# Four input loads moved earlier on the SyncE queue of a convolution and maxout kernel

## The chip, the core and the metric

The kernel runs on one core of a Trainium2 chip. The metric is the device time of one execution in microseconds. The kernel before took 485.3 us, the median of 11 runs that lay between 483.31 and 487.07.

The core has five engines that matter here: TensorE (PE in the profile, with its weight loads as PEld), VectorE (DVE), ScalarE (ACT), GpSimd (POOL) and SyncE (SP), which only issues transfers. Each takes its instructions in the order in which the program wrote them. An instruction that waits holds up all that stands behind it on the same engine.

## The reference

The input x has 8 batches of 4160 rows of 192 values. Each of 8 heads (24 columns) is filtered along the rows by 7 weights, which are the softmax of that head's row of `weight`. The result goes through a maxout layer with 768 hidden units and an output matrix:

```
w = softmax(weight)                        # 8 heads x 7 taps
y[b, s, h, :] = sum_k w[h, k] * xpad[b, s + k, h, :]      # 6 zero rows ahead of each batch
h = max(max(y @ w1, y @ w2), y @ w3)       # 33280 x 768
out = h @ w_out                            # 33280 x 192, float32
```

## The kernel before

The 33280 rows are cut into 65 blocks of 512. 64 of them lie within one batch; the last is made of the eight remainders of 64 rows. Blocks are numbered t.

The way of one block through the core:

- `load_x(t)` (line 133) brings x to SBUF as float32, in chunks of 112 rows that overlap, so that each holds the rows its filter needs. It is one transfer of 420 KB, or two (168 and 252 KB) where the block begins a batch, as blocks 0 and 8 do. All loads are issued by SyncE. Blocks 0 to 5 have buffers of two small pools of their own; from block 6 on the loads go round the four buffers of `xfp`.
- `cast_x(t)` (line 149) turns it to float16 on GpSimd.
- `conv(t)` (line 295) does the filter as 40 small matmuls with a band matrix, into two PSUM tiles.
- `evac(t, i)` (line 335) copies the two PSUM tiles to SBUF as `ys`, one by ScalarE and one by VectorE.
- `repack(t)` (line 348) puts the heads' columns in order by six SBUF to SBUF transfers, `yd<-ys`, three issued by SyncE and three by GpSimd.
- `double(t)` (line 354) copies the 64 filled partitions to the other 64 by one transfer of 192 KB, `yd<-yd`, issued by SyncE. It must wait until all six pieces have landed.
- `l1(t, j)` (lines 365 to 370), for j from 0 to 5, is the first layer for 128 hidden units: six matmuls, a Relu on ScalarE, a maximum on VectorE. It reads both halves of `yd`.
- `st2(t, u)` (line 409) is the second layer in six parts, and `store` (line 435) writes the result.

Blocks 0 to 2 are treated otherwise: their casts leave gaps for heads so that the convolution gives the right columns at once (`conv_dense`, line 314). Block 2's duplicate is made by two transfers that SyncE issues at lines 482 and 483, once its convolution has been copied out of PSUM.

No scheduler reorders anything: the order of calls in the source is the order on each engine. After a start-up part written out by hand, the loop `for t in range(2, NB)` (line 508) runs iteration t: the first layer of block t mixed with the second layer of block t - 1. On even t it also runs the convolutions of blocks t + 3 and t + 4, and in the first few iterations small tables say which blocks are loaded, cast, convolved, repacked and doubled: iteration 2 convolves blocks 4 and 5, iteration 3 block 6, iteration 4 blocks 7 and 8. From iteration 4 on `load_x(t + 6)` opens each iteration, and must wait for a cast to free its buffer. In iterations 2 and 3 the loads of the table `loads_at` stand behind the repacks:

```
    loads_at = {2: (7,), 3: (8, 9)}
    casts_at = {2: (6,), 3: (7, 8)}
    convs_at = {2: (4, 5), 3: (6,)}
    repacks_at = {2: (4,), 3: (5, 6)}
    doubles_at = {2: (), 3: (4,), 4: (5, 6)}
```

Of the kernel before, what the change touches and what calls it, by code (L numbers as in the profile page):

```python
# [27 lines left out]
def kernel(  # L28
# [84 lines left out]
    def load_x(t, eng=nc.sync):  # L113
        if not 0 <= t < NB:
            return
        chunks = chunks_of[t]
        n = len(chunks)
        pool, tag = (xfp, "xf") if t > 5 else ((xap, "xa") if t in (0, 3, 5) else (xbp, "xb"))
        xf = (pool.tile([P, NQ, D], FP32, tag=tag, name=f"xf_{t}") if n <= NQ else
              const.tile([P, n, D], FP32, name=f"xf_{t}"))  # L120
        parts = []
        i, n = 0, len(chunks)
        row = [c[1] * SEQ + c[2] for c in chunks]
        while i < n:
            k = i
            while (k + 1 < n and chunks[k + 1][3] == chunks[i][3]
                   and row[k + 1] - row[k] == row[i + 1] - row[i]):
                k += 1
            step = row[i + 1] - row[i] if k > i else 0
            rlen = chunks[i][3]  # L130
            src = bass.AP(tensor=x.tensor, offset=row[i] * D,
                          ap=[[D, rlen], [step * D, k - i + 1], [1, D]])
            eng.dma_start(out=xf[0:rlen, i:k + 1, :], in_=src)
            if parts and parts[-1][0] == rlen:
                parts[-1] = (rlen, parts[-1][1], k + 1)
            else:
                parts.append((rlen, i, k + 1))
            i = k + 1
        xin[t] = [xf, None, parts]
# [48 lines left out]
    load_x(1)  # L188
    load_w(2)
    nc.sync.dma_start(out=wos[:], in_=moe_w_out.rearrange("(j p) c -> p j c", p=P))  # L190
    for t in range(2, 6):
        load_x(t)

    ident = const.tile([P, P], FP32)
# [146 lines left out]
    def repack(t):  # L341


        if t >= NB:
            return
        yd = dense[t] = ydp.tile([P, NC, NBLK], FP16, tag="yd", name=f"yd_{t}")
        for n, (half, s0, c, r0, rows) in enumerate(pieces):
            (nc.sync, nc.gpsimd)[n % 2].dma_start(out=yd[r0:r0 + rows, c, :],  # L348
                                                  in_=slots[t][s0:s0 + rows, half, :])

    def double(t):

        if NDENSE <= t < NB:
            nc.sync.dma_start(out=dense[t][HALF:P, :, :], in_=dense[t][0:HALF, :, :])

    def l1(t, j):


        N, y = blkN[t], dense[t]
        ps = [pool.tile([P, NBLK], FP32, tag=tag, name=f"l{tag}_{t}_{j}")  # L360
              for pool, tag in ((psp, "p"), (psq, "q"))]
        for c in range(NC):
            for i in range(2):
                row = slice(HALF * i, HALF * (i + 1))
                nc.tensor.matmul(ps[i][:, 0:N], lhsT=wd[row, c, P * j:P * (j + 1)],  # L365
                                 rhs=y[row, c, 0:N],
                                 start=(c == 0), stop=(c == NC - 1))
        r = rp.tile([P, NBLK], FP16, tag="r", name=f"r_{t}_{j}")
        nc.scalar.activation(out=r[:, 0:N], in_=ps[0][:, 0:N], func=AF.Relu)  # L369
        nc.vector.tensor_max(out=hs[t][:, j, 0:N], in0=r[:, 0:N], in1=ps[1][:, 0:N])  # L370
# [110 lines left out]
    conv_dense(2, (nc.scalar.copy, nc.vector.tensor_copy, nc.scalar.copy), PQ)  # L481
    nc.sync.dma_start(out=dense[2][HALF:P, 0:NC:2, :], in_=dense[2][0:HALF, 0:NC:2, :])
    nc.sync.dma_start(out=dense[2][0:HALF, 1, :], in_=dense[2][HALF:P, 1, :])
    l1(1, 4)
    st2(0, 2, NJ)
    st2(0, 3, NJ)
# [4 lines left out]
    cast_x(4)  # L491
    cast_x(5)
    repack(3)
    load_x(6)
    double(3)
    l1(1, 5)
    st2(0, 4, NJ)
# [2 lines left out]

    loads_at = {2: (7,), 3: (8, 9)}
    casts_at = {2: (6,), 3: (7, 8)}
    convs_at = {2: (4, 5), 3: (6,)}
    repacks_at = {2: (4,), 3: (5, 6)}
# [62 lines left out]
```

The softmax here doesn't subtract the row's maximum and nothing guards it: scores larger than these inputs give would overflow.

## Time and profile before

| what | value |
|---|---|
| median of 11 runs | 485.3 us |
| the profiled execution's own time | 485.75 us |
| its span, first to last instruction | 483.8 us |
| TensorE busy | 468.4 us (97%) |
| VectorE, ScalarE, GpSimd busy | 76%, 67%, 44% |
| mean granted clock of TensorE | 0.992 |
| x loads, 420 KB each: median from issue to landing | 4.8 us |
| `yd<-yd` of 192 KB: median from issue to landing | 3.4 us |

The span is measured in one profiled execution; every time of a row is counted from its start. In a row of the table of groups, the first number after the bar is the time that the group was busy, the second the mean duration in nanoseconds, and after the next bar stands the time that the engine sat idle just before, with what ended it. "PEclk" or the granted clock is the share of TensorE's full clock that it was given. In a row of a timeline stand the start, the duration (of all that was merged in the row), the engine, the line, the operation, the tile written and read, the count, and in brackets the idle time before it. A DMA row on SPq or POOL is the issue of a transfer; it lands later. Matmuls are pipelined, so a busy TensorE is not one at its peak.

### The profile page before, as it was taken

The page shows a single profiled execution, that of the slowest core. Times are in us where ns is not written, and L with a number is a line of the kernel's source. Part 1 is how long each engine was busy: PE and PEld are TensorE (multiplying, and loading weights), DVE is VectorE, ACT ScalarE, POOL GpSimd, SP SyncE. Part 2 cuts the span into 40 slices and gives each one's busy share as a digit, 9 for nine tenths or more (in the row PEclk, how much of TensorE's full clock was granted, in tenths as well). Part 3 has the DMA queues.
Part 4 walks back from the last instruction along what each step waited for, and adds up shares of the span by engine and source line. Part 5 has one row for each costly group of instructions (what it writes and reads, how often), then busy time and mean ns, then how long its engine had stood idle before and what let it go on. Part 6 is the DMA issues. An engine that isn't in the chain of part 4 may idle for free.

```text
span 483.8 us, 21790 instructions
## 1 busy us (share of the span) xinstructions
PE 468.4 (97%) x9008; PEld 392.3 (81%) x9008; DVE 368.8 (76%) x612; ACT 323.8 (67%) x602; POOL 213.4 (44%) x346
## 2 busy tenths in 40 slices
PE   8799799999999999999999999999999999999996
PEld 4377588888888888888888888888888888888995
DVE  7777377778777787778787778777787778787774
ACT  4666376767676767676676766676766676666764
POOL 3644354345345534543554345345525543454200
PEclk9999799999999999999999999999999999999999
DMA  9746866676666667666666676575657766664423
GB/s 193 178 137 164 222 161 173 180 202 164 166 181 184 171 161 201 175 177 173 172 186 170 176 200 168 161 203 155 182 160 182 188 180 181 176 181 115 104 66 99
DMA packets 68576, 81.86 MB, mean 169 GB/s; under 512 B 9422, under 2 KB 57486, under 8 KB 68478
## 3 DMA queue, kind: packets, MB, share of 16 engines
q1 hardware_dynamic: 55310, 49.51, 41.5%
q0 software_dynamic: 13008, 30.88, 20.7%
q8 instruction: 70, 1.15, 1.1%
q14 instruction: 28, 0.23, 0.2%
q10 hardware_dynamic: 160, 0.10, 0.1%
HBM read 30.31 MB, written 25.56 MB: 115 GB/s over the span
## 4 chain that ended last, share of the span: by engine, by line
PE 94%; DVE 2%; ACT 1%; DMA 1%; issue 0%; SPq 0%; POOL 0%; ACTq 0%; POOLq 0%; DVEq 0%
PE lp L365 31%; PE po L409 30%; PE lq L365 25%; PE G L295 7%; DMA xf<-in_x_dram 1%; PE D L314 1%; DVE h L370 1%; ACT r L369 0%; PE idle L211 0%; DVE line L228 0%; ACT L225 0%; DVE wd L250 0%; PE band_cols L232 0%; DVE yd L330 0%; POOL x L149 0%
## 5 line engine op out<-in xcount | busy, mean ns | idle before, releaser
L370 DVE TENSOR_TENSOR h<-r,lq 128x512 f16<-128x512 f16 x390 | 267.1, 685 | 101.3 <-ACT r L369 101.0
L369 ACT ACTIVATE r<-lp 128x512 f16<-128x512 f32 x390 | 232.9, 597 | 141.0 <-PE lp L365 92.8
L365 PE MATMUL lp<-yd,wd 64*128 64x512 f16 x1170 | 316.9, 378 | 2.0 <-DVE wd L250 1.6
L365 PE MATMUL lq<-yd,wd 64*128 64x512 f16 x1170 | 315.8, 376 | 1.7 <-DVE h L370 1.7
L409 PE MATMUL po<-wo,h 64*128 64x192 f16 x3120 | 231.5, 243 | 0.0
L409 PEld LDWEIGHTS <-h 64*128 64x128 f16 x3120 | 186.9, 94 | 26.0 <-issue 0.5
L365 PEld LDWEIGHTS <-wd 64*128 64x128 f16 x2340 | 164.6, 94 | 26.7 <-issue 4.7
L435 POOL DMA_DIRECT2D out_dram<-o x63 | 49.9, 792 | 232.8 <-DVE o L419 221.7
L348 POOL DMA_DIRECT2D yd<-ys x186 | 94.0, 509 | 4.6 <-ACT ys L335 2.1
L409 PE MATMUL po<-m,yd 64*128 64x192 f16 x780 | 87.4, 244 | 0.0
L419 DVE TENSOR_TENSOR o<-a,po 128x384 f32<-128x384 f32 (+1 forms) x132 | 71.4, 542 | 0.6 <-ACT a L418 0.6
L149 POOL CAST x<-xf 112x960 f16<-112x960 f32 x61 | 60.7, 995 | 11.9 <-DMA xf<-in_x_dram 11.9
L418 ACT COPY a<-po 128x384 f32<-128x384 f32 (+1 forms) x132 | 61.6, 468 | 1.4 <-PE po L409 1.4
L409 PEld LDWEIGHTS <-yd 64*128 64x128 f16 x780 | 54.9, 94 | 8.5
L295 PEld LDWEIGHTS <-x 112*32 112x32 f16 x2440 | 29.4, 97 | 18.1 <-issue 13.3
L335 DVE CAST ys<-G 128x512 f16<-128x512 f32 x62 | 39.8, 682 | 5.0 <-PE G L295 5.0
L295 PE MATMUL G<-band,x 112*32 112x103 f16 (+1 forms) x2440 | 34.5, 210 | 4.6 <-POOL x L149 4.6
L335 ACT CAST ys<-G 128x512 f16<-128x512 f32 x62 | 33.6, 588 | 6.8 <-PE G L295 5.5
L166 POOL CAST xz<-xf 112x240 f16<-112x240 f32 (+2 forms) x12 | 3.6, 346 | 7.7 <-DMA xf<-in_x_dram 7.7
L211 PE MATMUL idle<-idle 128*128 128x512 f16 x10 | 4.6, 629 | 1.2 <-DVE idle L206 1.2
L314 PEld LDWEIGHTS <-xz 112*32 112x32 f16 x180 | 3.6, 111 | 1.4 <-DVE w3s L254 0.8
L314 PE MATMUL D<-band,xz 112*32 112x103 f16 (+1 forms) x180 | 4.1, 236 | 0.0
(48 smaller groups left out, 43.1 us busy)
## 6 DMA issues: line engine op xcount, KB each, us to landing
out_dram<-o POOLq DMA_DIRECT2D x63, 384.0 KB, 4.0
xf<-in_x_dram SPq DMA_DIRECT2D x57, 420.0 KB, 4.8
yd<-yd SPq DMA_DIRECT2D x62, 192.0 KB, 3.4
yd<-ys SPq DMA_DIRECT2D x62, 48.0 KB, 3.6
yd<-ys POOLq DMA_DIRECT2D x62, 48.0 KB, 3.6
xf<-in_x_dram SPq DMA_DIRECT2D x8, 252.0 KB, 3.4
yd<-ys SPq DMA_DIRECT2D x62, 32.0 KB, 3.3
yd<-ys POOLq DMA_DIRECT2D x62, 32.0 KB, 3.9
```

Of the source, the lines that this page charges most:

```text
L149: nc.gpsimd.tensor_copy(out=v[0:rl, q0:q1, :], in_=xf[0:rl, q0:q1, :])
L295: nc.tensor.matmul(G[i][32 * g:32 * g + 32, lo:hi], lhsT=x16[0:rlen, cb:cb + 32], rhs=band[0:rlen, h, cc:cc + hi - lo], start=True, stop=T ...
L314: nc.tensor.matmul(ps[32 * g:32 * g + 32, lo:hi], lhsT=xz[t][0:rlen, q, v, 32 * s:32 * s + 32], rhs=band[0:rlen, h, cc:cc + hi - lo], star ...
L335: copy(out=slots[t][:, i, :], in_=convs[t][i][:])
L348: (nc.sync, nc.gpsimd)[n % 2].dma_start(out=yd[r0:r0 + rows, c, :], in_=slots[t][s0:s0 + rows, half, :])
L365: nc.tensor.matmul(ps[i][:, 0:N], lhsT=wd[row, c, P * j:P * (j + 1)], rhs=y[row, c, 0:N], start=(c == 0), stop=(c == NC - 1))
L369: nc.scalar.activation(out=r[:, 0:N], in_=ps[0][:, 0:N], func=AF.Relu)
L370: nc.vector.tensor_max(out=hs[t][:, j, 0:N], in0=r[:, 0:N], in1=ps[1][:, 0:N])
L409: nc.tensor.matmul(ps[b0, i][:, s % 2, :], lhsT=a, rhs=b, start=first, stop=last)
L418: nc.scalar.copy(out=a[:, ss, :], in_=ps[s0, 0][:, ss, :])
L419: nc.vector.tensor_add(out=outs[t][:, s0:s + 1, :], in0=a[:, ss, :], in1=ps[s0, 1][:, ss, :])
L435: qs[i].dma_start(out=bass.AP(tensor=out.tensor, offset=r * D, ap=[[D, n], [step * D, s1 - s0], [1, D]]), in_=ob[p0:p0 + n, s0:s1, :])
```

## The change

Four loads are issued earlier on SyncE. The load of x6 comes directly after x5's. The load of x7 comes after the two transfers of lines 482 and 483, ahead of `repack(3)`. The load of x8 stands where x6's was, between `repack(3)` and `double(3)`. The load of x9 stands where x7's was, behind `repack(4)` in iteration 2. Iteration 3 loads nothing any more. No instruction is added or taken away, and the casts, convolutions and everything on the other engines keep their order.

```diff
-    for t in range(2, 6):
+    for t in range(2, 7):
         load_x(t)
...
     nc.sync.dma_start(out=dense[2][0:HALF, 1, :], in_=dense[2][HALF:P, 1, :])
+    load_x(7)
     l1(1, 4)
...
     repack(3)
-    load_x(6)
+    load_x(8)
     double(3)
...
-    loads_at = {2: (7,), 3: (8, 9)}
+    loads_at = {2: (9,)}
```

## The prediction

> **What bounds the kernel now.** I began with the page's table of groups, and there with the column of idle time. TensorE is busy 97% of the span, and of its matmul groups only the convolution of line 295 sat idle for microseconds; the cast of line 149 ended that idle time.
>
> ```profile
> L295 PE MATMUL G<-band,x 112*32 112x103 f16 (+1 forms) x2440 | 34.5, 210 | 4.6 <-POOL x L149 4.6
> ```
>
> The view of waits from 26 us to the end has that wait of 4.6 us once, and no other matmul row in it. So behind the start-up TensorE never stops except there, and what is won or lost on TensorE comes out at the end one for one. The timeline of TensorE shows the place (start, duration, what, count, idle time before it):
>
> ```profile
> 31.87 1.10 PE L295 MATMUL G<-band,x 112*32 112x103 f16 x80
> ...
> 35.45 0.38 PE L365 MATMUL lp<-yd,wd 64*128 64x512 f16 x1
> ...
> 38.63 0.38 PE L365 MATMUL lp<-yd,wd 64*128 64x512 f16 x1
> ...
> 46.73 0.64 PE L295 MATMUL G<-band,x 112*32 112x103 f16 x40
> 52.01 1.05 PE L295 MATMUL G<-band,x 112*32 112x103 f16 x40 [4.64 <-POOL x L149]
> ...
> 57.04 0.38 PE L365 MATMUL lp<-yd,wd 64*128 64x512 f16 x1
> ```
>
> At 31.87 block iteration 2 runs its two convolutions (blocks 4 and 5) in one piece. At 46.73 iteration 4 runs the same pair for blocks 7 and 8: block 7's forty matmuls end at 46.73 + 0.64 = 47.37, block 8's start at 52.01. The chain of work that ended last, between 46 and 53 us, says why:
>
> ```profile
> 46.90 0.58 SPq L133
> ...
> 47.53 3.29 DMA xf<-in_x_dram
> ...
> 50.96 1.00 POOL x L149
> ```
>
> x8 (in two transfers, being cut at a batch's end) was issued only at 46.90 and 47.53, landed at 50.82, and its cast ended at 51.96. Why so late is read on SyncE's own timeline, which issues in program order:
>
> ```profile
> 14.46 8.84 SPq L133 DMA_DIRECT2D xf<-in_x_dram  x4
> 28.20 0.63 SPq L482 DMA_DIRECT2D yd<-yd  x1
> 28.93 0.56 SPq L483 DMA_DIRECT2D yd<-yd  x1
> 30.29 1.85 SPq L348 DMA_DIRECT2D yd<-ys  x3
> 32.18 0.60 SPq L133 DMA_DIRECT2D xf<-in_x_dram  x1
> 35.67 0.51 SPq L354 DMA_DIRECT2D yd<-yd  x1
> ...
> 41.52 5.33 SPq L348 DMA_DIRECT2D yd<-ys  x6
> 46.90 2.15 SPq L133 DMA_DIRECT2D xf<-in_x_dram  x4
> 49.22 1.23 SPq L354 DMA_DIRECT2D yd<-yd  x2
> ```
>
> x8's load stands behind the six moves of blocks 5 and 6 (41.52 to 46.85), the last of which wait for block 6's evacuation. x6 went at 32.18, x7 at 38.14, so the prefetch is one place too short by iteration 4. The stretches of 4 us show the second cost, in the column after POOL's (granted clock):
>
> ```profile
> 48.00:52.00 4.00, 0.00 (x0) 0.00 (x0) 0.06 (x1) 0.00 (x0) 1.04 (x2) 0.66 0.89 230
> 52.00:56.00 4.00, 4.00 (x68) 2.96 (x70) 1.38 (x3) 1.18 (x2) 2.74 (x5) 0.50 1.05 262
> 56.00:60.00 4.00, 4.00 (x61) 2.95 (x57) 2.77 (x5) 2.16 (x4) 0.38 (x1) 0.99 0.65 188
> ```
>
> TensorE does nothing, its clock falls to half, and stays there until 56.1 after it resumes.
>
> **The change part by part.** It adds no instruction; it moves four loads, five DMA issues, on SyncE. All four buffers of the pool are empty at the start, so none of x6 to x9 waits for a cast; x10 waits for x6's cast as before.
>
> *What is removed.* Take the same stretch in both iterations, from the pair's first matmul to the group l1 3: iteration 2 took 35.45 - 31.87 = 3.58 us, iteration 4 took 57.04 - 46.73 = 10.31. The difference, 6.73 us, is the whole price: 4.64 idle and 2.09 of half clock (conv 8 took 1.05 where iteration 2's second half took 1.10 - 0.64 = 0.46, so 0.59; from the pair's end to l1 3, 57.04 - 53.06 = 3.98 against 35.45 - 32.97 = 2.48, so 1.50). Both iterations step by 1.06 us per group after that, so nothing more is hidden there.
>
> *x8, to the place of x6.* It is issued after repack(3), at 32.18 and about 32.8. x6 took 4.5 us from there, so x8 is in by about 37. What is late next is GpSimd: its queue holds x8's cast behind x7's, which runs 44.26 to 45.25 after the moves of blocks 5 and 6. x8's cast then ends at 46.25; conv 8 can start at 47.37. It is hidden by 1.1 us. x9 takes x7's place at 38.14; its own cast comes in iteration 4 and its convolution in iteration 6, no risk.
>
> *x6, behind x5.* x5's issue ends at 23.30, SyncE then waits until 28.20 for conv 2: x6's issue (about 0.6 us) fits with 4 us to spare. In 27 to 29 us the DMA engines are nearly idle in the windows (16 and 0 GB/s), so x6 is in at 28 to 29.3 (x5, the one just before, took 4.8 us from issue, and x4 to x5 was 1.9 us). Next behind it are the two moves of dense 2, landed at 30.60 and 30.95 for the group at 31.08. Cost 0 to 0.4 us; I take 0, since their packets start near 29.3.
>
> *x7, between the moves of dense 2 and repack(3).* SyncE is free from 29.49 to 30.29, the issue takes 0.6: nothing on SyncE. But its 420 KB now run ahead of repack(3). That repack's last pieces landed at 35.6 and 35.4, and only then could double(3) go, at 35.67. The first group of iteration 3 reads it at 38.63 without waiting. This duplicate has no landing in the trace; others of line 354 took 2.7 us at least, so it was in between 38.37 and 38.63: **at most 0.26 us of cover.** [...] The row: a load such as x6 has 4.5 us from issue to landing, so x7 is in at about 34.0, and the pieces (80 KB, landing at best 2.0 us after issue) follow within half a microsecond, still ahead of 35.6. [...] By the row it is 0 to 0.6. I take 0.3: the rate between 31 and 34 us was 50 to 133 GB/s, where 380 was reached at 35, so there is room for it; the other half of the repack goes by GpSimd's queue.
>
> *Iteration 4's SyncE.* x8 and x9 are gone from it, so x10 goes at 46.90, double(5) at about 47.5, double(6) at about 48.3, when repack(6) has landed (48.2). With the stall gone, iteration 5's first group is at 46.73 + 1.10 + 0.36 + 5.30 = 53.49 (the last two are the gap and the run l1 1 to the next iteration's l1 0 of iteration 2). double(5) lies behind x10 in the queue: x10 in at 51.4 (4.5 us) to 52.7 (5.8, as x9 took among others), then 192 KB at 230 GB/s, 0.8 us: 52.2 to 53.5. Cost 0 to 0.3 us; with it as slow as double(6) was (7.7 us), 1.7. I take 0.1.
>
> *The sum.* 6.73 - 0.3 - 0.1 = 6.3 us. The profiled execution took 485.75 us (span 483.8 and 1.95 around it): 485.75 - 6.3 = 479.4. It lay 0.45 above the median of the runs, so against the median 485.3 - 6.3 = **479.0 us**, 1.3% less.
>
> *The clock.* [...] The rows say 2.09, and that the clock was down by 49.3, 1.9 us after TensorE stopped (0.64 granted between 49 and 50). [...]
>
> **The rivals.**
> *A, the forecast:* the stall goes, new waits sum to under 1 us: 478.5 to 479.6. For it: the one wait of the waits view, and 1.1 us of cover behind it.
> [...]
> *C, no change:* x8's cast is held by something else on GpSimd, and conv 8 waits as long. 485.3. Against it: GpSimd stood idle for 5.71 us ahead of that cast, waiting for the load alone.
> *D, slower:* x7 ahead of repack(3) delays its landing by a whole load, 2.3 us, so double(3) goes at 37.9, and behind x8 it takes 7.7 us as double(6) did: 45.6, 7.0 us after 38.63. That idle time drops the clock too, 2.1: 485.3 - 6.7 + 9.1 = 487.7. It decides from a wait of 4.7 us at iteration 3. Against it: at 36 to 38 us one load, not three, is in the queue.
>
> **How the numbers follow.** A 0.74, B 0.19, C 0.03, D 0.04. Two tenths of a percent (1.0 us) is about what a measurement of this kernel can tell from no change; A and B are faster by more: 0.93. Same 0.03, slower 0.04. The range begins at 485.3 - 6.9 - 0.6 = 477.8 (no new wait, and a median half a microsecond off, as the eleven runs from 483.31 to 487.07 let it be) and ends at 481.6, within B.
>
> **What would show it.** Right: the matmul row of line 295 loses its 4.6 us; the pair of iteration 4 stands as one row of 80, as in iteration 2; the granted clock stays at full from 48 to 56 us; the cast of line 149 no longer waits 5.7 us for its load. [...] Wrong: a wait above 1.9 us before iteration 3's first group with half clock after it, or GpSimd's cast of x8 ending later than 47.4.

## The result and the profile after

The changed kernel took 480.13 us, the median of 12 runs between 478.63 and 482.77. The ratio to the kernel before, run in the same rounds, is 0.9896, with a 95% interval of 0.988 to 0.9911: about 5.0 us, or 1.0%, faster. The forecast was 479.0 us with a range of 477.8 to 481.6.

The profiled execution took 479.65 us, its span is 477.8. In the page's table of groups, the convolution has lost its idle time, and the cast waits for loads 4.2 us in all where it waited 11.9:

```profile
L149 POOL CAST x<-xf 112x960 f16<-112x960 f32 x61 | 60.6, 995 | 4.2 <-DMA xf<-in_x_dram 4.2
...
L295 PE MATMUL G<-band,x 112*32 112x103 f16 (+1 forms) x2440 | 33.9, 209 | 0.0
```

TensorE's timeline, at the places that the prediction named (start, duration, what, count, idle time before it):

```profile
31.58 1.10 PE L295 MATMUL G<-band,x 112*32 112x103 f16 x80
...
39.32 0.64 PE L295 MATMUL G<-band,x 112*32 112x103 f16 x40
...
46.45 1.10 PE L295 MATMUL G<-band,x 112*32 112x103 f16 x80
...
50.03 0.38 PE L365 MATMUL lp<-yd,wd 64*128 64x512 f16 x1
...
54.35 0.39 PE L365 MATMUL lq<-yd,wd 64*128 64x512 f16 x1 [0.77 <-DMA yd<-ys]
```

Blocks 7 and 8 are convolved in one piece of 80. From there to the group l1 3 it takes 50.03 - 46.45 = 3.58 us, the figure of iteration 2 to the hundredth. But the last row is a wait that the kernel before did not have, in iteration 5's first group, which reads block 5's duplicate. The row names a piece of a repack as what ended it; the piece that landed then, issued at 49.82, is of block 7, which this group does not read. I take the wait to be for the duplicate. SyncE's timeline shows that duplicate in its new company:

```profile
41.27 5.79 SPq L348 DMA_DIRECT2D yd<-ys  x6
47.15 0.53 SPq L133 DMA_DIRECT2D xf<-in_x_dram  x1
48.21 1.56 SPq L354 DMA_DIRECT2D yd<-yd  x2
```

The load of x10 is issued at 47.15, the duplicates of blocks 5 and 6 behind it at 48.21 and 48.93. The granted clock (the column after POOL's) stays full:

```profile
48.00:52.00 4.00, 4.00 (x63) 3.04 (x61) 3.23 (x6) 2.44 (x6) 2.71 (x5) 1.00 0.81 244
52.00:56.00 4.00, 3.23 (x49) 2.33 (x46) 2.38 (x5) 2.09 (x4) 0.93 (x2) 1.00 0.83 220
```

In these two profiles the span falls by 6.0 us, in the medians the time falls by about 5.0.

### The profile page after: what moved, and what is told of

Its sections match the earlier page's. It is cut to its first block, busy times and chain, and to the rows that moved or that the text cites. A ratio compares the mean times of both kernels' runs of the same rounds, so it can differ in the third digit from the quotient of the medians.

```text
span 477.8 us, 21790 instructions
## 1 busy us (share of the span) xinstructions
PE 466.6 (98%) x9008; PEld 390.0 (82%) x9008; DVE 367.8 (77%) x612; ACT 323.9 (68%) x602; POOL 213.5 (45%) x346
## 3 DMA queue, kind: packets, MB, share of 16 engines
q8 instruction: 70, 1.15, 1.1%
## 4 chain that ended last, share of the span: by engine, by line
PE 95%; DVE 2%; ACT 1%; DMA 1%; issue 0%; ACTq 0%
PE lp L365 31%; PE po L409 30%; PE lq L365 26%; PE G L295 7%; DMA yd<-ys 1%; PE D L314 1%; DVE h L370 0%; PE idle L211 0%; ACT r L369 0%; DVE wd L250 0%; ACT L225 0%; PE band_cols L232 0%; DVE yd L330 0%; DVE line L228 0%; ACT w3s L254 0%
## 5 line engine op out<-in xcount | busy, mean ns | idle before, releaser
L250 DVE TENSOR_TENSOR wd<-ws,w3s 128x768 f16<-128x768 f32 (+1 forms) x4 | 3.4, 854 | 1.2 <-DMA ws<-in_moe_w_dram 1.1
```

## The experiments

To compare profiles I use one measure, taken from the rows of line 295 in TensorE's timeline: the way from the start of the convolutions of blocks 4 and 5 to that of blocks 9 and 10. It covers iterations 2 to 5, and its parts are A (to block 6's convolution), B (from there to block 7's) and C (from block 7's on). "Loss" is what the whole way took above 28.80 us, the shortest seen. (B takes 7.27 us where nothing waits, and 7.13 right behind a wait in A, which gives 0.14 back.) Work on TensorE is the same in all but the two kernels with fillers.

| profile | A | B | C | loss, us |
|---|---|---|---|---|
| the kernel before, first | 7.59 | 7.27 | 20.68 | 6.74 |
| the kernel before, again (3 more) | 7.59, 8.20, 7.58 | 7.26, 7.13, 7.27 | 16.78, 19.72, 19.00 | 2.83, 6.25, 5.05 |
| the changed kernel, first | 7.74 | 7.13 | 15.01 | 1.08 |
| the changed kernel, again (2 more) | 8.65, 8.34 | 7.20, 7.13 | 14.35, 20.21 | 1.40, 6.88 |
| duplicates first in iteration 4 | 8.37 | 7.56 | 13.95 | 1.08 |
| x8 alone moved | 7.60 | 7.97 | 16.11 | 2.88 |
| x7 and x8 ahead of repack(3) | 10.83 | 7.13 | 13.94 | 3.10 |
| 20 fillers | 7.59 | 7.26 | 18.49 | 4.54 |
| 14 fillers | 7.59 | 7.27 | 17.84 | 3.90 |
| each load up by one place (2) | 7.59, 7.59 | 7.27, 7.27 | 13.94, 13.94 | 0, 0 |

**Duplicates first.** The changed kernel, with iteration 4's duplicates ahead of x10's load.

```diff
-        if t > 3:
+        if t > 4:
             load_x(t + 6)
             cast_x(t + 5)
         for u in doubles_at.get(t, (t + 2,)):
             double(u)
+        if t == 4:
+            load_x(t + 6)
+            cast_x(t + 5)
```

> The changed kernel with one more move: in iteration 4 the duplicates of blocks 5 and 6 are issued ahead of the load of x10, not behind it. My theory is that the new wait of 0.77 us ahead of iteration 5's second group (at 53.6 us) is the duplicate of block 5 queued behind x10's load. Then the wait goes, x10 is issued about 2 us later without harm (its cast comes in iteration 5), and the time is 0.7 to 1.0 us under the changed kernel's, 479.3 us. The rival: the duplicate is late because the pieces of repack(5) landed late (one only at 47.97), which this order does not mend; then the wait stays at 0.5 us or more and the time is that of the changed kernel, 480.1.

Measured: 480.34 us, ratio 0.9911 (0.9883 to 0.9939). C is 13.95 us, so the wait of iteration 5 is gone, though the duplicate of block 5 was itself issued late, at 49.14. But A and B lost 0.78 and 0.29 in this execution, to the duplicates of blocks 3 and 4. The mechanism is as I had it, the gain is not: the median is that of the changed kernel. In the one execution that was profiled, other waits took the place of the one that went; that this holds for the median is not shown.

**x8 alone.** The kernel before, with x8 directly behind x7.

```diff
-    loads_at = {2: (7,), 3: (8, 9)}
+    loads_at = {2: (7, 8), 3: (9,)}
```

> The kernel before with x8's load alone moved, to directly behind x7's in iteration 2; x6, x7 and x9 stay where they were. If the stall of iteration 4 hangs on x8's place alone, the 4.6 us of idle time and the half clock behind it go, 6.7 us. But x9 and x10 are then issued one after the other ahead of the duplicate of block 5, two loads of about 2 us each in front of it instead of one: I expect it to land between 54.5 and 56.5 us where 53.5 is needed, a wait of 1 to 3 us, and 480.3 to 482.5 us in all, about 481.4. The rival, that x9's place does not matter (its cast and convolution are needed late), gives the changed kernel's 480.1 or less.

Measured: 480.14 us, ratio 0.9907 (0.9882 to 0.9932). The stall ahead of block 8's convolution is gone by this one move. The profile (481.8 us, the slowest of its six runs) has the waits that I expected of it: 0.70 us in B, where x7 and x8 stand in front of block 4's duplicate, and 2.17 in C, where x9 and x10 stand in front of block 5's. The median, though, is as good as the changed kernel's on the same chip (480.14 both), so those waits are hardly paid in full in most executions, and of the four moves x8's is the one that brings the gain.

**The clock's share.** The kernel before, with matmuls on zeros between the convolutions of blocks 7 and 8, first 20 and then 14 of them.

```diff
         for n, u in enumerate(us):
+            if u == 8:
+                keep_warm(20)      # 14 in the second kernel
             conv(u, PQ if n else ((psw, "w"), (psw, "w")))
```

> The kernel before, with 20 matmuls on a tile of zeros put on TensorE between the convolutions of blocks 7 and 8, so that TensorE works (about 4.3 us at full clock) while it waits for x8; their result is read by nobody. The wait for x8 stays as long as it was. If the half clock after the stall is the stall's second price, of 2.09 us, the clock stays full from 48 to 56 us and the time falls by 2.1 us to 483.2. The rival, that block 8's convolution and the groups behind it were slow for another reason (the DMA traffic of those microseconds), leaves 485.3.

> As the kernel before with fillers between the convolutions of blocks 7 and 8, but 14 matmuls, about 3.0 us, in place of 20. With 20 they ended 0.9 us after x8's cast (50.77 against 51.65), which ate part of the gain. With 14 TensorE is idle for at most 1.6 us, and nothing is held up. If the half clock is paid in most executions of the kernel before, the time falls by 1.5 to 2.1 us, a ratio of 0.9957 to 0.9969. If it is paid in the profiled one and few others, the ratio is 0.998 or more.

With 20: 484.11 us, ratio 0.999 (0.9975 to 1.0005). With 14: 482.78 us, ratio 0.995 (0.9929 to 0.997), so 1.5 to 3.4 us faster. The timelines, 20 first:

```profile
46.65 0.64 PE L295 MATMUL G<-band,x 112*32 112x103 f16 x40
47.23 4.49 PE L211 MATMUL idle<-idle 128*128 128x512 f16 x20
51.65 0.64 PE L295 MATMUL G<-band,x 112*32 112x103 f16 x40
```

```profile
47.02 0.64 PE L295 MATMUL G<-band,x 112*32 112x103 f16 x40
47.59 3.19 PE L211 MATMUL idle<-idle 128*128 128x512 f16 x14
51.37 0.64 PE L295 MATMUL G<-band,x 112*32 112x103 f16 x40 [0.58 <-POOL x L149]
```

In both, block 8's forty matmuls take 0.64 us and not 1.05, and the granted clock stays full. The row with 14, from 48 to 52 us, has it beside a DMA share of 0.94:

```profile
48.00:52.00 4.00, 3.42 (x55) 1.63 (x55) 0.35 (x1) 0.26 (x1) 1.67 (x2) 1.00 0.94 259
```

With 14, x8 still comes late, no useful work fills the wait, and 2.4 us are won: this is the clock's price by itself, beside the 2.09 of the prediction. The rival, that the groups were slow because of the DMA traffic, falls with it: the traffic is still there (a DMA share of 1.08 from 52 to 56 us, and 1.05 in the kernel before). Twenty fillers took 4.5 us, and x8's cast had ended 0.9 us before block 8's convolution began, so most of the gain was eaten; I expected 2.1 of it and the first count was too high.

**The kernel before, three more profiles.**

> The kernel before once more, for a second profile of the stall of iteration 4. The first had 4.64 us of idle time and 2.09 of half clock. If the sum of the prediction was right there, both come again within half a microsecond; if the stall differs from one execution to the next, as x8's landing does (50.82 in the first profile, 49.63 in the one with 20 fillers), the idle time lies nearer to 3.5 us, or the clock does not fall.

> The kernel before, a third profile of the stall of iteration 4, after 6.7 us (4.64 idle, the rest at half clock) and 2.8 (2.65 idle, no fall of the clock). If the stall's length hangs on when x8 lands, the idle time lies between 2.5 and 5 us again, and the clock falls only where it is above about 3 us.

> The kernel before, a fourth profile of the same stall: idle time between 2.5 and 5 us, with half clock behind it only where it is above about 3 us. A median price of all four between 4.5 and 6 us would match the 5.2 us by which the changed kernel and the one with each load moved by one place are faster.

They took 481.58, 484.2 and 484.59 us. TensorE's timeline of each at block 8's convolution:

```profile
49.76 0.64 PE L295 MATMUL G<-band,x 112*32 112x103 f16 x40 [2.65 <-POOL x L149]
```

```profile
50.72 0.65 PE L295 MATMUL G<-band,x 112*32 112x103 f16 x40 [3.97 <-POOL x L149]
```

```profile
51.21 1.05 PE L295 MATMUL G<-band,x 112*32 112x103 f16 x40 [3.37 <-POOL x L149]
```

The stall is no constant. Its idle time was 4.64, 2.65, 3.97 and 3.37 us, and the first profile, on which the prediction's sum rests, was the longest of the four. The clock stayed full behind the one of 2.65 and fell with the other three. The four losses, 6.74, 2.83, 6.25 and 5.05, have a median of 5.65 us; about 0.5 of the 6.25 is a wait in A, for block 3's duplicate.

**Two loads ahead of the repack.** The changed kernel, with x8 moved up to x7, so that both are in the queue in front of repack(3).

```diff
     load_x(7)
+    load_x(8)
     l1(1, 4)
...
     repack(3)
-    load_x(8)
     double(3)
```

> The changed kernel with x8's load ahead of repack(3) too, directly behind x7's, so that two loads and not one stand in front of that repack's pieces on SyncE's queue. In three profiles the way from the convolution of blocks 4 and 5 to that of block 6 took 7.59 us (the kernel before), 7.74 and 8.65 (the changed kernel twice). If x7 in front of the pieces is what makes the duplicate of block 3 late, a second load in front adds its transfer of some 2 us: that way takes 9.6 to 11 us, and the time is 1 to 3 us above the changed kernel's, 481 to 483. The rival, that the duplicate's lateness is chance traffic, leaves that way at 7.6 to 8.7 us and the time at 480.1.

Measured: 483.49 us, ratio 0.9976 (0.9956 to 0.9995), so 3.4 us above the changed kernel's first measurement. SyncE's timeline, and TensorE's:

```profile
29.68 1.67 SPq L133 DMA_DIRECT2D xf<-in_x_dram  x3
31.45 1.85 SPq L348 DMA_DIRECT2D yd<-ys  x3
37.79 0.50 SPq L354 DMA_DIRECT2D yd<-yd  x1
```

```profile
42.03 0.39 PE L365 MATMUL lq<-yd,wd 64*128 64x512 f16 x1 [2.95 <-DMA yd<-yd]
```

The three pieces are issued by 33.30, the last of them landed at 37.65, and only then could the duplicate go, 2.1 us later than in the first profile of the kernel before. A is 10.83 us. With no load ahead of the repack A is 7.58 to 7.60 in eight profiles and 8.20 in one; with one it is 7.74 to 8.65 in four; with two it is 10.83. So x7 in front of the pieces does make block 3's duplicate late. The issue of that duplicate shows it more sharply. Here are its rows in the third profile of the changed kernel, then in the second of the last kernel below, where no load is ahead:

```profile
36.71 0.51 SPq L354 DMA_DIRECT2D yd<-yd  x1
```

```profile
33.82 0.51 SPq L354 DMA_DIRECT2D yd<-yd  x1
```

Counted from the start of the convolutions of blocks 4 and 5, it goes after 2.44 to 2.52 us in seven of the nine profiles with no load ahead, after 3.80 and 3.92 in the other two (the first of the kernel before and x8 alone), after 4.18 to 5.11 in the four with one load and after 5.84 with two. The profile that the prediction was read from was one of the two late ones.

**The changed kernel, twice more.**

> The changed kernel once more, on the same chip as its neighbours: 480.1 us, and how far the new wait ahead of iteration 5's second group (0.77 us in its first profile) varies from one execution to another. My theory, that it is a queue of transfers with some cover, lets it lie between 0 and 1.5 us; none of over 1.9, since the clock would fall with it.

> The changed kernel beside the run with each load moved by one place: 480.1 us, with 1.0 to 1.5 us of waits between the convolutions of blocks 4 and 5 and those of blocks 9 and 10 in its profile. Those waits come from the queue in front of a duplicate; the rival, that the two are the same, gives 479.3 to 479.6.

Measured: 480.14 us, ratio 0.9907 (0.9889 to 0.9925), and in the last set of runs 481.13 us, ratio 0.9925 (0.9899 to 0.995). The first has its waits in A (1.06 us). The second's profiled execution took 485.71 us, no less than the kernel before, which I had not expected. TensorE's timeline of it, then the step of the chain that ended last, then its clock:

```profile
57.53 0.60 PE L365 MATMUL lq<-yd,wd 64*128 64x512 f16 x1 [3.02 <-DMA yd<-yd]
```

```profile
49.35 8.13 DMA yd<-yd
```

```profile
56.00:57.00 1.00, 0.00 (x0) 0.00 (x0) 0.00 (x0) 0.00 (x0) 1.00 (x2) 0.87 1.09 282
57.00:58.00 1.00, 0.47 (x4) 0.20 (x6) 0.00 (x0) 0.00 (x0) 1.00 (x2) 0.50 1.03 289
```

Block 5's duplicate went at 49.35, behind x10's load of 48.58, and was waited for until 57.48. TensorE stood 3.02 us, its clock fell to half and was still there at 63 us. This is much like the old stall, at another place: the loss is 6.88 us. A time as long is rare: of the 29 runs of the changed kernel two are above 483 us, and only this one was profiled.

**Each load up by one place.** The kernel before, with no load put ahead of a repack, and iteration 4's duplicates first.

```diff
-    for t in range(2, 6):
+    for t in range(2, 7):
         load_x(t)
...
-    load_x(6)
+    load_x(7)
     double(3)
...
-    loads_at = {2: (7,), 3: (8, 9)}
-    casts_at = {2: (6,), 3: (7, 8)}
+    loads_at = {2: (8,)}
+    casts_at = {2: (6,), 3: (7, 8), 4: (9,)}
...
-        if t > 3:
+        if t > 4:
             load_x(t + 6)
             cast_x(t + 5)
         for u in doubles_at.get(t, (t + 2,)):
             double(u)
+        if t == 4:
+            load_x(9)
+            load_x(10)
```

> The kernel before with each load moved up by one place only, each behind the repack and not ahead of it: x6 behind x5 at the start, x7 where x6 was, x8 where x7 was, and in iteration 4 the duplicates of blocks 5 and 6 first, then x9 and x10; x9's cast goes behind the repack of block 7. Then the stall of iteration 4 is gone and no load stands newly in front of a duplicate that is due soon. If the changed kernel's missing microsecond is such new waits (1.2 and 1.5 us in its two profiles), they go: 0 to 0.3 us of waits in iterations 3 to 5, and 478.9 us, 1.2 under the changed kernel. The rival, that the missing microsecond is a stall that was smaller in most executions than in the profiled one, gives 480.1.

> Each load moved up by one place, once more, beside the changed kernel on one chip. In its first profile no wait was left in iterations 3 to 5 and its six runs lay between 478.92 and 480.05. If the changed kernel pays for waits of about a microsecond in most executions, this one is 0.5 to 1.2 us under it here too, and its runs lie closer together. If the waits of the changed kernel's profiles are made good elsewhere, the two agree within 0.3 us.

Measured: 479.32 us, ratio 0.9893 (0.9867 to 0.9918), and 478.99 us, ratio 0.987 (0.984 to 0.99). In both profiles no wait is left in iterations 2 to 5. SyncE's timeline of the second shows the order:

```profile
39.48 4.92 SPq L348 DMA_DIRECT2D yd<-ys  x6
44.93 3.00 SPq L354 DMA_DIRECT2D yd<-yd  x2
47.98 1.81 SPq L133 DMA_DIRECT2D xf<-in_x_dram  x2
```

Its twelve runs lie between 478.27 and 480.05 us; the changed kernel's 29 spread from 478.60 to 485.71. On the chip that ran both, the medians are 478.99 and 481.13, 2.1 us apart, though the intervals of the ratios just touch. On that chip it is the better kernel of the two. The two first medians, of different chips, are only 0.8 us apart, and their ratios agree (0.9893 and 0.9896). Above all it is the steadier one.

## Why the prediction was right, and where its sizes were off

The direction and the mechanism of the gain held: the stall ahead of block 8's convolution is gone with its half clock. The sum of 6.3 us was 1.1 to 1.3 too large. The range held because its upper end, 481.6, lies in rival B, that late duplicates take back part of the gain. What they can take at the worst was my estimate, and no run shows that bound: in the three profiles of the changed kernel the loss was 1.08, 1.40 and 6.88 us. The case that was given 0.74, new waits under 1 us and 478.5 to 479.6 us, did not come. Both sizes in the sum erred the same way: the stall was taken too large, the new waits too small.

*What is removed.* In the profile that was read, 6.73 us was exact: the changed kernel runs the same stretch in 3.58 us. For the typical run it is too large. I subtracted the profiled execution's stall from the median of the runs, as if each run had it, though that execution was 0.45 us above the median. How much too large is not settled by the four losses and their median of 5.65: the three later executions (481.58, 484.2 and 484.59 us) are 3.3, 1.3 and 0.9 us under the medians measured beside them, so that sample is on the low side. The kernel with no waits left measures the stall better: it is faster by 5.2 us at one time and 6.3 at another. So 0.4 to 1.5 us of the 6.73 is not there in the typical run. The new waits, for which I had 0.4, are what the changed kernel's medians lie above that kernel's: 0.8 us between two chips, 2.1 on one.

*The clock.* A term of its own, as the 14 fillers show: 2.4 us (1.5 to 3.4) against 2.09. My reading of when it falls was not safe. I took from one row that 1.9 us of standing can be enough. Waits of 2.65 and 2.95 us went without a fall; waits of 3.02, 3.37, 3.97 and 4.64 had one. The rows of the granted clock, first of the kernel before, then of its third profile, show two of the falls:

```profile
49.00:50.00 1.00, 0.00 (x0) 0.00 (x0) 0.00 (x0) 0.00 (x0) 0.00 (x0) 0.64 0.78 220
```

```profile
51.00:52.00 1.00, 1.00 (x42) 0.88 (x32) 0.57 (x1) 0.59 (x1) 0.40 (x1) 0.61 1.13 290
```

The first came 1.9 us after TensorE stopped, the second 4.5 us after, when it had already resumed; the other two, read from rows like these, came 2.2 and 3.2 us after. From fall to rise the half clock lasted 6.8 us in the first profile of the kernel before and in the bad execution, and 3.4 in the other two. The idle time before a fall had no such fixed length: the clock fell 1.9 us into one wait, and behind the one of 3.02 only 2.2 us after TensorE stopped. What decides whether and when it falls is not shown by these runs. That the clock's price is a probability for waits of this length is my guess; six waits, which also sort by their length at about 3.0 us, do not prove it.

*x8 to the place of x6, cover on GpSimd.* Right: x8's cast follows x7's at once, and block 8's convolution follows block 7's without a gap in all three profiles.

*x6 behind x5.* Right: it landed at about 28.5, and the way from block 3's convolution to that of blocks 4 and 5 was 2.85 us before and after.

*x7 ahead of repack(3).* The cost was named, the size was low. The 0.3 in the sum was my estimate, and no run shows it; A lost 0.15, 1.06 and 0.75 us. Two readings failed. The 0.26 us of cover was that of a profile in which the pieces were late by themselves; in most the duplicate goes 1.3 us earlier, so there was more cover, and x7 took more than it: the duplicate went 1.7 to 2.6 us later than in most profiles with no load ahead. And the other half of the repack, on GpSimd's queue, was no help: its pieces of 32 and 48 KB took 4.2 to 5.0 us from issue to landing in the three profiles of the changed kernel, and 1.8 to 3.7 in five with no load ahead. So the place behind x7 on SyncE's queue does not explain the delay alone. The page of the kernel before counts the packets of the two large queues against the same 16 DMA engines (41.5% and 20.7% of their time), and the engines' share from 32 to 33 us rose from 0.55 to 1.06; no run separates the two causes. (SyncE's three pieces are 96 KB, of 48, 32 and 16, and not 80.)

*double(5) behind x10.* I took 0.1 with 1.7 as the worst. It was 1.07 in the first profile, 0.41 and 6.27 in the others (C above 13.94). Two things failed. The duplicate was not issued at 47.5 but at 48.21, since pieces of repack(5) landed only at 47.97. And what goes behind x10 is slow (6.0 us from issue to landing is the median of the two duplicates in the first profile, and block 5's took 8.13 in the bad execution), while the DMA engines are all but fully used (0.81 to 0.83, and 0.92 to 1.17 in each microsecond from 51 to 56 in the bad execution). That x10's place matters rests on one pair of profiles: with the duplicates first, block 5's was issued 1.05 us after block 7's convolution began, against 1.15 in the second profile of the changed kernel, and nothing was lost where 0.41 was. In the two profiles of the last kernel it also went ahead of that convolution, so they show the cure and not which part of it works. Nor does x10 in front always cost: with two loads ahead of repack(3) the duplicate went behind x10 too, but 0.16 us after that convolution began, and C was at its floor. What drew out the duplicate of 8.13 us, of the traffic in it, was not singled out.

So the case that came was rival B, part of it comes back, and not A; C did not happen. D's mechanism, a new wait long enough to cost the clock and the whole gain, does exist, but at iteration 5 and not at 3, and only in some executions. D's 2.3 us for a whole load was an estimate; in the profile that was read, x5's cast started 1.9 us behind x4's, each as its load landed. The new waits are 1.1 to 1.4 us in two profiles where I had 0.4. (The range's lower end subtracts 6.9 where the sum has 6.73; with that it is 478.0.)

## What to carry to other kernels

A load that is moved up to mend one late transfer can push back the small transfers issued behind it (block 3's duplicate went 1.7 to 2.6 us later), here also those on another queue (4.2 to 5.0 us from issue to landing, and not 1.8 to 3.7): move it by the smallest step that covers the stall, and not ahead of a transfer that is due sooner. A stall that is read off one profile is one draw; before it is subtracted from a median, look at a second and third profile of the same kernel. And steadiness is a result: the order with no waits left gained 0.8 and 2.1 us in the median over the changed kernel, and its slowest run of twelve, 480.05 us, is no slower than the changed kernel's median.

## What had not been expected

The same program's stall varied from 2.65 to 4.64 us of idle time, and the clock made of that a loss of 2.8 to 6.7 us. Half clock lasted until 56.1 us in the first profile of the kernel before, 4.1 us after TensorE resumed, and about 6 us after it in the bad execution of the changed kernel. A single duplicate of 192 KB, which takes 3.4 us in the median, took 8.13 behind one load of 420 KB.
